# Two loads of one tile pair placed apart in the SyncE queue of a long-convolution and soft-MoE kernel

## The chip, the cores and the metric

The kernel runs on one core of one Trainium2 chip. The metric is device time of one launch in microseconds (us). Before the change three runs took 909.78, 915.08 and 910.25 us; their median is 910.25 us.

## What is computed

The input `x` has 8 batches of 5696 positions and 128 channels. It is convolved along the positions with a filter `h` as long as the sequence (in the reference by a Fourier transform of twice the length, causal part kept); the result, 45568 rows of 128, goes through a soft mixture of experts with 32 slots.

```python
def _attn_ref(x, h):
    L = 2 * S
    Xf = np.fft.rfft(x, n=L, axis=1)
    Hf = np.fft.rfft(h, n=L, axis=0)
    y = np.fft.irfft(Xf * Hf[None, :, :], n=L, axis=1)[:, :S, :]
    return y

def _moe_ref(x, phi, w1, w2):
    logits = x @ phi
    d = softmax(logits, axis=0)
    slot_input = (d.T @ x).reshape(E, S_per_e, D)
    for e in range(E):
        slot_out[e] = np.maximum(slot_input[e] @ w1[e], 0.0) @ w2[e]
    c = softmax(logits, axis=1)
    return c @ slot_out
```

(The two `softmax` calls stand for the reference's maximum, exponential and sum.) All arithmetic is 32-bit floating point.

## The kernel before, in words

The transform is done by matrix products in two levels, 90 by 64. Nine groups are run through it: group 0 is the filter, groups 1 to 8 are the batches. Between the levels the data goes through internal tensors in DRAM, because the axis that lies across the partitions changes.

- **Stage a** (`stage_a`, matmuls L241, evictions L243): folds and transforms eight chunks a group. It is called once a step for the low 60 frequencies and in every odd step also for the high 30 of two chunks. Its stores go to `f` (L225): two of 240 KB for the low part ("f60" below) and four of 120 KB for the high part ("f30" below). The input comes by `load_x` (tile `xc`, 768 KB, L198).
- **Stage b** (`load_g` L270, `stage_b1` L284, `stage_b2` L327 and L332): twelve units a group. A unit is loaded as `gt` (512 KB), transformed, multiplied by the filter's spectrum, transformed back and evicted as `zst`. The first eight units of a group are stored to `zm` (two stores of 256 KB), the last four to `zr` (four stores of 128 KB, or of 32 KB for the very last one). `load_g` of a group can run only when all of that group's `f` is written.
- **Stage c** (`stage_c1` to `stage_c6`): pairs of chunks, four pairs a batch, 32 in all. Pair T needs two loads: `load_main` brings 64 of the 90 frequencies (tile `zc` from `zm`, 1 MB, L374), `load_rest` the other 26 (tile `zx` from `zr`, 512 KB, L385). In `stage_c1` the matmuls of L412 read `zc`, and directly behind them on TensorE the matmuls of L417 read `zx` and add to the same banks. There is one buffer of each for the steady part. What follows from a pair are token rows, logits, both softmaxes and the accumulation of the slots' inputs.

**The order is written out by hand.** One loop over steps t = 0 to 80 issues for every step a piece of stage a, one to two units of stage b and a piece of stage c, and each engine runs its instructions in the order in which the loop issued them. `LAG_C` = 27: `stage_c1` of pair T is in the odd step 27 + 2T. `pair(-2)` in an odd step is the pair whose `stage_c1` comes two steps later, `pair(-1)` in an even step the pair whose `stage_c1` comes in the next step. `NQ` = 4, so `T % NQ == 0` is the first pair of a batch, whose `zr` data is written late.

**All steady loads and stores are issued by SyncE, in one queue.** Stores are not issued where they arise: `stage_a` and `stage_b2` append them to `pending`, and `flush()` issues what is there. Every DMA of the program takes the next of eight completion semaphores in turn and, before it is issued, waits for the DMA that used this semaphore eight DMAs earlier. SyncE is held meanwhile, with all that is queued behind.

In an odd step the queue gets: the two f60 stores (first `flush()`), `zc` of the pair two steps on, `zx` of the same pair directly behind it (unless it is the first of a batch), a `gt`, the stores of one unit, the four f30 stores (last `flush()`). In an even step: `zx` if the pair is the first of a batch, `xc`, the two f60 stores, `gt`, the stores of one unit (L225), a small store `c_t` (L562), another `gt`, the stores of another unit. After step 80 a tail without stages a and b runs the last pairs, the experts and the output.

Of the kernel before, what the change touches and what calls it, by code (L numbers as in the profile page):

```python
# [70 lines left out]
def kernel(  # L71
# [41 lines left out]
    NQ = NJ // 2  # L113
# [53 lines left out]
    def bank():  # L167
        rings.append(rings.pop(0))
        return rings[-1].tile([P, 512], F32, name="bank", tag="bank")
# [39 lines left out]
    def fold(c):  # L209
        if c not in xs:  # L210
            return
        t_ = xs.pop(c)
        y_ = xf[c % len(xf)]
        i = CH * (c % 2)
        near, far = t_[:, 0, i:i + CH, :], t_[:, 1, ::-1, :][:, i:i + CH, :]
        for o in range(2):
            nc.gpsimd.tensor_tensor(out=y_[:, o, :, :], in0=near, in1=far,  # L217
                                    op=AL.subtract if o else AL.add)
        folded[c] = y_
# [3 lines left out]
    def flush():  # L223
        while pending:
            pending.pop(0)()  # L225
# [38 lines left out]
    def load_g(u):  # L264
        if u >= (B + 1) * NW:
            return
        g, w, us = parts(u)
        n = sum(k for _, k in us)
        t_ = bpool.tile([P, 4, 2, D], F32, name="gt", tag="gt", bufs=3)
        nc.sync.dma_start(  # L270
            out=t_[:, 0:n, :, :].rearrange("p q c d -> p q (c d)"),
            in_=fd[g][8 * w:8 * w + 2 * n].rearrange("(q a) r c d -> (a r) q (c d)", a=2))
        gs[u] = t_
# [42 lines left out]
    def stage_b2(u):  # L316
        g, w, us = parts(u)
        if g == 0:
            return
        m = len(us)  # L320
        y_ = prods.pop(u)
        bz = bps.tile([P, 2, 2, 2 * D], F32, name="bz", tag="bz")
        for o, (i, n) in enumerate(us):
            for q in range(n):
                r = slice(q * HP, (q + 1) * HP)
                for a in range(2):
                    nc.tensor.matmul(bz[a * HP:(a + 1) * HP, q, o, :], vt[r, i, a, :],  # L327
                                     y_[r, a * m + o, :, :].rearrange("p c d -> p (c d)"),
                                     start=True, stop=True)
        n = us[0][1]  # L330
        st = bpool.tile([P, 2, 2, 2 * D], F32, name="zst", tag="zst", bufs=3)
        nc.scalar.activation(st[:, 0:m, 0:n, :].rearrange("p o q x -> p q o x"),  # L332
                             bz[:, 0:n, 0:m, :], AF.Copy)
        k = m * n
        sv = st[:, :, :, :].rearrange("p o q x -> p (o q) x")
        for o in range(2):
            if 8 * w < MAIN:
                pending.append(partial(
                    nc.sync.dma_start,
                    out=zm[g - 1][o, 8 * w:8 * w + 2 * k].rearrange("(q a) r c d -> (a r) q (c d)", a=2),  # L340
                    in_=sv[o::2, 0:k, :]))
                continue
            k0 = 8 * w - MAIN
            for c in range(2):
                pending.append(partial(
                    nc.sync.dma_start,
                    out=zr[g % 2][o, c, k0:k0 + 2 * k].rearrange("(q a) r d -> (a r) q d", a=2),
                    in_=sv[o::2, 0:k, c * D:(c + 1) * D]))
# [30 lines left out]
    def load_rest(T):  # L379
        if T >= NT:  # L380
            return
        b, j = divmod(T, NQ)
        t_ = zs[T]
        n = 2 * CH
        nc.sync.dma_start(  # L385
            out=t_[1][:, :, :, :].rearrange("p h n d -> p (h n d)"),
            in_=zr[(b + 1) % 2].rearrange("o c k r d -> (o c k) r d")[:, j * n:(j + 1) * n].rearrange(
                "p r x -> p (r x)"))
# [46 lines left out]
    def stage_c2(T):  # L435
        for k in (3, 1, 0, 2) if tail else (3, 2, 1, 0):
            p = bank()
            for i in range(CH):
                nc.tensor.transpose(p[:, i * TR:(i + 1) * TR], ys[T][0:TR, k * CH + i, 0:D],  # L439
                                    ident[0:TR, 0:TR])  # L440
            nc.scalar.activation(yt[:, k * CH:(k + 1) * CH, :, :], of_tokens(p), AF.Copy)  # L441
# [78 lines left out]
    def dispatch(T):  # L520
        ap_ = bank()
        d_ = ds.pop(T)
        y_ = ys.pop(T)
        for i in range(CH):
            for k in range(Q):
                r = slice(k * NSL, (k + 1) * NSL)
                nc.tensor.matmul(ap_[r, 0:D + 1], d_[:, i, r], y_[:, k * CH + i, :],  # L527
                                 start=(i == 0), stop=(i == CH - 1))
        if T == 0:
            nc.vector.tensor_copy(out=acc[:, :], in_=ap_[:, 0:D + 1])  # L530
        else:
            nc.vector.scalar_tensor_tensor(out=acc[:, :], in0=acc[:, :],
                                           scalar=scales.pop(T)[:, 0:1], in1=ap_[:, 0:D + 1],
                                           op0=AL.mult, op1=AL.add)
# [68 lines left out]
    def units(t):  # L603
        g, i = divmod(t - LAG_B, NJ)
        if t < LAG_B or g > B:
            return []
        return [g * NW + k for k in range(sum(PER[:i]), sum(PER[:i + 1]))]
# [23 lines left out]
    for t in range(last_front + 1):  # L631
        us = list(units(t))

        def pair(lag):
            T, half = divmod(t - LAG_C - lag, 2)
            return T if half == 0 and 0 <= T < NT else None

        def prefetch(last):
            nonlocal loaded
            while loaded < len(queue) and queue[loaded][0] <= last \  # L640
                    and queue[loaded][0] // NW * NJ + NJ <= t:
                load_g(queue[loaded][0])
                loaded += 1

        def slot_b(due=True):
            fresh = due and bool(us)
            if fresh:
                u = us.pop(0)
                stage_b1(u)
                prefetch(u + AHEAD)  # L650
                wait_b2.append(u)
            if len(wait_b2) > fresh:
                stage_b2(wait_b2.pop(0))

        T, U, V, W, X = [pair(k) for k in (0, 2, 1, 3, 5)]
        if t < NA:
            stage_a(t, False)
            fold(t + 1)
        if t == last_front:
            assert T is None and U is None  # L660
            assert pair(-1) % NQ
            flush()
            dispatch(W)
            for i in range(3):
                slot_b()
                flush()
                if i == 1:
                    softmax_sum(W)
                    stage_c2(V)
            assert not us and not wait_b2  # L670
            stage_c6(X)
            stage_c3(V)
            column_max(V)
            break
        if t % 2:
            if T is not None:
                stage_c1(T)()
            flush()
            if pair(-2) is not None:
                load_main(pair(-2))  # L680
                if pair(-2) % NQ:
                    load_rest(pair(-2))
            slot_b()
            if U is not None:
                stage_c4(U)
            if t < NA:
                stage_a(t, True)
            if U is not None:
                stage_c5(U)
                softmax_exp(U)  # L690
            flush()
        else:
            if pair(-1) is not None and pair(-1) % NQ == 0:
                load_rest(pair(-1))
            if t < NA:
                load_x(t // 2 + 2)
            flush()
            if t == NJ:
                prefetch(AHEAD - 1)
            slot_b()  # L700
            if W is not None:
                softmax_sum(W)
                dispatch(W)
            flush()
            if V is not None:
                stage_c2(V)
            if X is not None:
                stage_c6(X)
            slot_b()
            if V is not None:  # L710
                stage_c3(V)
                column_max(V)
            flush()
        if t == NA:
            lead.close()
            wts = inner.enter_context(tc.tile_pool(name="wts", bufs=1, side="right"))
            w1s = wts.tile([P, E, F], F32, name="w1s")
        if NA < t <= NA + E:
            nc.sync.dma_start(out=w1s[:, t - NA - 1, :], in_=moe_w1[t - NA - 1])
# [213 lines left out]
```

## Time and profile before

| | |
|---|---|
| three runs | 909.78, 915.08, 910.25 us; median 910.25 |
| profiled execution, own time | 909.23 us |
| its span in the trace | 907.4 us |
| granted TensorE clock, mean | 0.903 of full speed |
| TensorE matmul | 760.2 us busy, 84% of the span, 8308 instructions |
| TensorE weight load | 387.7 us, 43% |
| VectorE | 601.4 us, 66% |
| ScalarE | 436.8 us, 48% |
| GpSimd | 399.8 us, 44% |
| DMA, SyncE's and ScalarE's queue | 275.74 MB, 89.7% of 16 engines' span |
| DMA, all | 278.33 MB, mean 307 GB/s |

The profiled execution is one run of the program; its span leaves out 1.8 us around the first and last instruction. A view of the trace gives for every instruction its start, its duration and, in square brackets, how long its engine was idle before it and who ended that. For SyncE, the duration is that of the issue, not of the transfer. A piece "DMA" in the chain of waits runs from the issue to the landing.

### The profile page before, as it was taken

How to read it: one execution, taken by the hardware profiler on the slowest of the kernel's cores; microseconds unless marked ns; L12 is line 12 of the kernel's file. 1: busy time of each engine (PE TensorE's matmuls, PEld its weight loads, DVE VectorE, ACT ScalarE, POOL GpSimd, SP SyncE). 2: the span in 40 equal slices, each digit the busy share in tenths (PEclk: the TensorE clock that was granted, in tenths of full speed). 3: DMA queues.
4: the chain of work that ended last, by engine and by line, in shares of the span. 5: the costliest groups of instructions: out<-in, count | busy, mean ns of one | idle time of the engine just before them, and what ended most of it. 6: DMA issues, size and time to landing. Idle time of an engine off the chain costs nothing.

```text
span 907.4 us, 21291 instructions
## 1 busy us (share of the span) xinstructions
PE 760.2 (84%) x8308; PEld 387.7 (43%) x8308; DVE 601.4 (66%) x896; ACT 436.8 (48%) x880; POOL 399.8 (44%) x353
## 2 busy tenths in 40 slices
PE   6857778689999989999998999799888877767893
PEld 2212233234444444444444444344444434344793
DVE  2029767568778867886877787678778766653552
ACT  2423234335556545665655655456544444563441
POOL 4634322444555655655655566456332224651000
PEclk9979889999999999999999999899988888766855
DMA  8989999999999999999999999999998768540798
GB/s 267 318 275 343 293 296 337 298 314 376 341 291 375 361 326 308 372 358 299 357 364 335 295 373 348 303 308 346 306 291 304 264 200 341 186 166 1 292 406 335
DMA packets 170443, 278.33 MB, mean 307 GB/s; under 512 B 13543, under 2 KB 128231, under 8 KB 165135
## 3 DMA queue, kind: packets, MB, share of 16 engines
q1 hardware_dynamic: 169336, 275.74, 89.7%
q10 hardware_dynamic: 1008, 1.25, 0.5%
q8 instruction: 66, 1.08, 0.5%
q14 instruction: 33, 0.27, 0.1%
HBM read 147.94 MB, written 129.00 MB: 305 GB/s over the span
## 4 chain that ended last, share of the span: by engine, by line
PE 47%; DMA 23%; ACT 8%; POOL 8%; DVE 6%; issue 6%; SPq 1%; ACTq 0%; DVEq 0%; POOLq 0%
PE bank L241 9%; DMA gt<-f 9%; PE bt L284 9%; PE bz L327 6%; POOL y L430 5%; PE bank L412 4%; DMA f<-fst 4%; PE op L886 3%; PE bank L439 3%; PE bank L417 3%; PE bank L448 2%; DMA zx<-zr 2%; ACT fst L243 2%; DMA out_dram<-o 2%; PE bank L527 2%
## 5 line engine op out<-in xcount | busy, mean ns | idle before, releaser
L241 PE MATMUL bank<-x,s 128*32 128x512 f32 (+1 forms) x1152 | 218.0, 620 | 12.9 <-POOL x L217 8.4
L217 POOL TENSOR_TENSOR x<-xc 128x512 f32<-128x512 f32 x144 | 180.4, 1278 | 107.2 <-PE bank L241 86.5
L284 PE MATMUL bt<-gt,wt 64*64 64x256 f32 x1620 | 125.0, 419 | 72.8 <-DMA gt<-f 33.0
L430 POOL TENSOR_TENSOR y<-y,op 128x512 f32<-128x512 f32 x64 | 77.6, 1213 | 206.8 <-DVE op L404 204.3
L304 DVE TENSOR_TENSOR pi<-bt,Hi 128x1024 f32<-128x1024 f32 x96 | 113.0, 1177 | 83.5 <-PE bt L284 83.3
L243 ACT ACTIVATE fst<-bank 128x512 f32<-128x512 f32 x216 | 122.8, 592 | 86.0 <-PE bank L241 57.7
L332 ACT ACTIVATE zst<-bz 128x1024 f32<-128x1024 f32 x96 | 93.3, 972 | 128.3 <-PE bz L327 109.4
L284 PEld LDWEIGHTS bt<-gt,wt 64*64 64x64 f32 x1620 | 58.3, 141 | 151.2 <-issue 79.1
L312 DVE TENSOR_TENSOR yf<-bt,pi 128x512 f32<-128x512 f32 x192 | 119.4, 663 | 3.3
L304 DVE TENSOR_TENSOR bt<-bt,Hr 128x1024 f32<-128x1024 f32 x96 | 113.0, 1177 | 0.0
L241 PEld LDWEIGHTS bank<-x,s 128*32 128x32 f32 (+1 forms) x1152 | 55.1, 126 | 129.8 <-issue 93.6
L327 PE MATMUL bz<-yf,vt 64*64 64x256 f32 x1440 | 110.4, 404 | 0.0
L327 PEld LDWEIGHTS bz<-yf,vt 64*64 64x64 f32 x1440 | 64.3, 143 | 25.5 <-issue 4.2
L512 POOL TENSOR_TENSOR L<-L,rs 128x512 f32<-128x512 f32 x32 | 33.5, 1048 | 91.6 <-DVE rs L511 66.4
L404 DVE TENSOR_TENSOR y<-bank,y 128x512 f32<-128x512 f32 x32 | 22.1, 692 | 76.7 <-ACT y L420 76.5
L439 PE MATMUL bank<-ident,y 109*128 109x109 f32 x512 | 62.7, 273 | 7.9 <-ACT yt L441 7.9
L504 ACT ACTIVATE L<-L 128x512 f32<-128x512 f32 x32 | 20.2, 630 | 94.7 <-POOL L L501 94.6
L430 POOL TENSOR_TENSOR y<-y,om 128x512 f32<-128x512 f32 x54 | 63.9, 1183 | 2.1
L439 PEld LDWEIGHTS bank<-ident,y 109*128 109x128 f32 x512 | 52.9, 149 | 19.4 <-POOL x L217 14.7
L412 PE MATMUL bank<-zc,im 64*64 64x512 f32 x480 | 60.8, 623 | 0.0
L441 ACT ACTIVATE yt<-bank 128x360 f32<-128x360 f32 x128 | 53.0, 482 | 7.7 <-PE bank L439 7.3
L420 ACT ACTIVATE y<-bank 128x512 f32<-128x512 f32 x32 | 19.1, 596 | 72.6 <-PE bank L417 72.6
(101 smaller groups left out, 862.5 us busy)
## 6 DMA issues: line engine op xcount, KB each, us to landing
gt<-f SPq DMA_DIRECT2D x99, 512.0 KB
f<-fst SPq DMA_DIRECT2D x144, 240.0 KB
zm<-zst SPq DMA_DIRECT2D x128, 256.0 KB
zc<-zm SPq DMA_DIRECT2D x30, 1024.0 KB
xc<-in_x_dram SPq DMA_DIRECT2D x32, 768.0 KB
f<-fst SPq DMA_DIRECT2D x144, 120.0 KB
out_dram<-o SPq DMA_DIRECT2D x16, 1024.0 KB
zx<-zr SPq DMA_DIRECT2D x30, 512.0 KB
```

The lines of the kernel that those rows point to most:

```text
L217: nc.gpsimd.tensor_tensor(out=y_[:, o, :, :], in0=near, in1=far, op=AL.subtract if o else AL.add)
L241: nc.tensor.matmul(p[i * m:(i + 1) * m, :], s1[:, g // B, q + o, cols], columns(c_, o), start=True, stop=True)
L243: nc.scalar.activation(st[:, :, q, :], p[:, :].rearrange("p (n d) -> p n d", d=D), AF.Copy)
L284: nc.tensor.matmul(bt[q * HP:(q + 1) * HP, a, o, :], wt[r, 2 * i + q, :], t_[r, 2 * o + q, :, :].rearrange("p c d -> p (c d)"), start=True ...
L304: nc.vector.tensor_tensor(out=p_, in0=pv, in1=h_, op=AL.mult)
L312: nc.vector.tensor_tensor(out=y_[r, 0:k, c, :], in0=pv[:, :, c, :], in1=pi[r, 0:k, 1 - c, :], op=op_)
L327: nc.tensor.matmul(bz[a * HP:(a + 1) * HP, q, o, :], vt[r, i, a, :], y_[r, a * m + o, :, :].rearrange("p c d -> p (c d)"), start=True, sto ...
L332: nc.scalar.activation(st[:, 0:m, 0:n, :].rearrange("p o q x -> p q o x"), bz[:, 0:n, 0:m, :], AF.Copy)
L412: nc.tensor.matmul(ps[o, c][h_ * HP:(h_ + 1) * HP, :], im[r, c, :], zt[r, h_, :, c, :], start=True, stop=False)
L430: eng.tensor_tensor(out=part_, in0=part(v, 0), in1=o_[:, :, :], op=sign)
L439: nc.tensor.transpose(p[:, i * TR:(i + 1) * TR], ys[T][0:TR, k * CH + i, 0:D], ident[0:TR, 0:TR])
L441: nc.scalar.activation(yt[:, k * CH:(k + 1) * CH, :, :], of_tokens(p), AF.Copy)
```

## The change

Two loads change their place in the step; their number, size and data do not.

- `load_main` in an odd step is now issued directly after `stage_c1`, ahead of the `flush()` that issues the two f60 stores.
- `load_rest` is no longer issued behind it. It is issued for all pairs alike in the following even step, after the `flush()` that issues the stores of that step's first unit, so behind `xc`, two f60 stores, `gt` and the unit's stores, and ahead of `c_t` and the second `gt`. In the step that opens a group there are two `gt` ahead of it.
- In the last step (t = 80), which has its own order, `load_rest` stands after `dispatch`.

```diff
@@ -661,6 +661,7 @@
             assert pair(-1) % NQ
             flush()
             dispatch(W)
+            load_rest(pair(-1))
             for i in range(3):
                 slot_b()
                 flush()
@@ -675,11 +676,9 @@
         if t % 2:
             if T is not None:
                 stage_c1(T)()
-            flush()
             if pair(-2) is not None:
                 load_main(pair(-2))
-                if pair(-2) % NQ:
-                    load_rest(pair(-2))
+            flush()
             slot_b()
             if U is not None:
                 stage_c4(U)
@@ -690,8 +689,6 @@
                 softmax_exp(U)
             flush()
         else:
-            if pair(-1) is not None and pair(-1) % NQ == 0:
-                load_rest(pair(-1))
             if t < NA:
                 load_x(t // 2 + 2)
             flush()
@@ -702,6 +699,8 @@
                 softmax_sum(W)
                 dispatch(W)
             flush()
+            if pair(-1) is not None:
+                load_rest(pair(-1))
             if V is not None:
                 stage_c2(V)
             if X is not None:
```

## The prediction

> **What bounds the kernel now.** I read the page's slices first, to find the stage that the change touches. The two moved loads run from 176 us (pair 0) to 770 us, slices 8 to 34 of 40.
>
> ```profile
> PE   6857778689999989999998999799888877767893
> ...
> DMA  8989999999999999999999999999998768540798
> ```
>
> TensorE and the DMA engines are both over 90% busy in slices 8 to 29. So neither name alone settles anything: the question is which waits for the other, and where. TensorE's waits between 170 and 665 us, then SyncE's own from 176 to 665 us (total, times, longest):
>
> ```profile
> PE bt L284 <- DMA gt<-f: 16.2, 6, 5.5
> ...
> PE bank L417 <- DMA zx<-zr: 2.5, 2, 2.3
> ```
>
> ```profile
> SPq L225 <- DMA gt<-f: 40.3, 47, 2.4
> SPq L225 <- DMA zc<-zm: 22.1, 22, 1.7
> ```
>
> TensorE loses 16.2 us to `gt` (each time the first one of a group) and 2.5 us to `zx` (2.28 of it at pair 0). SyncE mostly waits for landings eight DMAs back: its queue is full, and runs behind the data that it stores. How far behind, a regular pair shows (pair 10, whose matmuls of L417 need `zx`). Three timelines: ScalarE, SyncE, TensorE.
>
> ```profile
> 378.58 1.06 ACT L243 ACTIVATE fst<-bank 128x512 f32<-128x512 f32 x2
> ```
>
> ```profile
> 383.20 3.99 SPq L225 DMA_DIRECT2D f<-fst  x4
> 388.22 0.34 SPq L198 DMA_DIRECT2D xc<-in_x_dram  x1
> 389.61 1.44 SPq L225 DMA_DIRECT2D f<-fst  x2
> 391.14 0.41 SPq L270 DMA_DIRECT2D gt<-f  x1
> 391.64 1.64 SPq L225 DMA_DIRECT2D zm<-zst  x2
> 393.38 0.57 SPq L562 DMA_DIRECT2D c_t<-cst  x1
> ...
> 398.17 0.34 SPq L374 DMA_DIRECT2D zc<-zm  x1
> 398.91 0.43 SPq L385 DMA_DIRECT2D zx<-zr  x1
> ```
>
> ```profile
> 391.62 1.95 PE L412 MATMUL bank<-zc,im 64*64 64x512 f32 x16
> 393.50 1.11 PE L417 MATMUL bank<-zx,ir 26*64 26x512 f32 x16
> ```
>
> The f30 data is evicted at 378.58 + 1.06 = 379.64, its first store goes out at 383.20: 3.6 us behind, and 7.2 at the fourth. The chain of waits gives a landing in that stretch, from issue to end:
>
> ```profile
> 391.64 6.46 DMA zm<-zst
> ```
>
> Last, what a group's first `gt` costs, at its worst (TensorE's timeline):
>
> ```profile
> 583.22 1.99 PE L284 MATMUL bt<-gt,wt 64*64 64x256 f32 x16 [5.52 <-DMA gt<-f]
> ```
>
> **Part 1: `zc` ahead of the f60 stores.** No instruction is added. The two stores' bytes no longer land before it, so it lands about 1.2 us earlier (neighbouring landings of f60 lie 0.6 us apart). In pairs 0 to 27 it landed 3.0 us or more before L412 used it (landings: last step of the DMA's completion semaphore): gain 0. The new wait: SyncE now stands at `zc` until L412 of the pair before has read the buffer, and the f60 stores, `gt` and unit stores queue behind. In the rows above that wait is long over at the issue (L412 ran at 371.5, `zc` of pair 10 was issued at 378.8), so 0; with SyncE level with TensorE it is up to 1.6 us (f60 evicted 372.2, L412 done 373.4, 0.4 of issue), and nobody needs those stores before the f30 stores behind them: still 0.
>
> **Part 2: `zx` moved on.** In pair 10's step its new place is behind the second `zm` store. As the queue is full, what lands by a place is set by the bytes ahead of it. Ahead of the new place stands what stood ahead of that store before, `zx` included, so `zx` will land about when that store landed: 398.85 us. L417 needs it at 393.50: 5.35 late. The same subtraction for pairs 0 to 23 gives 3.4 to 9.3 us late (pair 0: 197.68 against 190.13, 7.55; pairs 1 to 7: 4.2 to 7.1; pair 16: 7.9; pair 19: 9.3; pair 20: 7.0; pair 23: 3.7), and 0.8 to 11 us to spare for 24 to 27, step 80 among them: 0 there.
>
> These latenesses don't add up. Once TensorE has waited about 7 us at pair 0, everything it makes comes 7 us later while the queue, which was that far behind, goes on. So **pair 0 costs 7.0 us** (6.5 if `zx`'s own wait for the last `zr` stores, about 1 us, is gained; 7.55 if not). Then SyncE is level with the data, and what counts is the shortest path from eviction to L417. Regular pair, zero at 379.64, L417 due at 13.86: four f30 issues of 0.44 (two unheld ones took 0.88), `xc` issued by 2.3 and landed 5.5 later (shortest such row: 325.61 to 331.13), 7.8; two f60 (evicted at 5.2, no hold), 0.6 each, 9.0; `gt` 1.4, 10.4; two `zm` of 0.65, 11.7; `zx` 1.3, **13.0**. It fits by 0.9: **regular pairs 0**. In the step that opens a group (pairs 3, 7, 11, 15, 19) there is a second `gt` and four `zr` of 0.36 stand for the two `zm`: 14.5 against 13.4, **1.1 late, five times, 5.5 us**. Bounds by `xc`: 6.3 if it lands 2.75 (its spacing to its predecessor) after the last f30 at 3.5, which leaves nothing late; 7.0 after its issue, as in long queues, which makes 2.6 late, and regular pairs 0.6.
>
> **What goes.** A TensorE that is late by several us finds the groups' first `gt` there. The stalls after pair 0 were 3.36, 2.07, 1.69 and 5.52: **-12.6 us**. Before the worst of them the delay left is 7.0 + 4 x 1.1 - 3.36 - 2.07 - 1.69 = 4.3, and pair 19's row asks for 9.3; 5.0 is open. The queue may have caught up by then (0) or not (5.0); I take 2.0, nearer to caught up, since a regular cycle holds about 18.9 us of transfers by their landing spacing, against TensorE's 20.15. Removed with `zx` from its old place: `xc` or a unit's stores no longer wait behind it; with TensorE the later one, 0.
>
> **What other DMAs pay.** Moved behind `zx` are `c_t` and the step's second `gt`, 1.3 us later at most; `gt` is loaded three units ahead, and outside group starts no wait for it is recorded: 0.
>
> Sum: 7.0 + 5.5 - 12.6 + 2.0 = **+1.9 us** on the profiled execution's 909.2 us, 911.1. The median of the runs is 1.0 above that execution: **912**.
>
> A rule of the Trainium skill speaks against the change: "DMA: Bandwidth & Descriptors", Rules for kernel authors, has a DMA issued early and waited for late, and `zx` is now issued some 13 us later; taken alone it would have every pair pay, where the rows make only pair 0 and group starts pay. The same page (Anatomy of one DMA) fits a DMA on GpSimd's path as 2.0 us plus bytes at 436 GB/s; as an estimate for `xc` that is 3.8 us where the rows have 5.5 and more, no pair but the first would be late, and the sum would be about -6.
>
> **Rivals.** (a) *The shortest path does not fit*: `zx` lands later than 13.86 us after the f30 eviction in regular pairs too. It decides from 0.9 us of extra latency on, such as `xc` rows of 7 us. One us late in 18 regular pairs and 2.1 at five group starts: 18 + 10.5 + 7.0 - 12.6 + 2.0 = +25, 935. For it: `xc` rows reach 7.1. Against: those stood in a full queue.
> (b) *It fits everywhere*: 6.5 + 0 - 12.6 + 0 = -6, 904. For it: the shorter landing of `xc`.
> (c) *No pair is late*, because the queue, with no two loads side by side, is never behind: the 2.3 us of pair 0 go, and 1.3 us at each of four `gt` stalls: -7.5, 903. For it: the DMA engines moved only 133 GB/s from 345.5 to 350 us, where `zx` waited for `zr`. Against: 24 rows that say late.
> (d) *The queue keeps the pace it had, and TensorE just follows*: pair 20's row, with no `gt` stall after it, leaves +7.0 at the end, 917. It is the upper part of the forecast, not a case apart.
>
> **How the numbers follow.** Forecast 0.57, (a) 0.23, (b) 0.15, (c) 0.05. A measurement of this kernel can tell about 1% from no change, 9.1 us. (b), (c) and nearly all of the forecast lie within it: faster 0.04, same 0.69, slower 0.27 ((a) and the forecast's bad end, boundaries at 2.6 and the 5.0 open). The range goes from (b), 904, to 926, which takes in the forecast's bad end and the milder half of (a): about 0.07 is left out below and 0.11 above.
>
> **What the profile of after would show.** TensorE's wait for `zx` at L417 grows from 2.5 us to 12 to 16: one wait of about 9 at pair 0 and about 1 at five group starts; more than 15 such waits mean (a), none means (c). The wait of L284 for `gt` falls from 16.2 to under 6. SyncE waits more for evictions (L243, L332) and less for `zc` and `gt` landings. From pair to pair L412 comes every 20.15 us. Wrong from the root would be: `zx` landing in its new place well before the store ahead of it did, or a period over 20.15 without a wait for a DMA.

## The result and the profile after

The changed kernel takes 1008.2 us (median of four runs, 1008.15 to 1008.72); the kernel before, run beside it, 910.01 (four runs, 908.73 to 915.08). The ratio is **1.107, 95% interval 1.103 to 1.111**: 98 us slower, where 912 was forecast with a range to 926. The profiled execution of the changed kernel has a span of 1006.4 us against 907.4, and a mean granted clock of 0.88 against 0.903.

The slices of the changed kernel's page, the same two rows as before:

```profile
PE   5758677678888878887988798878987877766893
...
DMA  8999999988888888888888888798888986652598
```

In slices 8 to 29 TensorE was at 9 in 16 of 22 and is now in 3; the DMA engines were in all 22 and are now in one. Both have become less busy at once, so neither is short of time: they wait for each other. TensorE's waits of the changed kernel between 170 and 665 us, then SyncE's between 176 and 665 us (total, times, longest):

```profile
PE bank L417 <- DMA zx<-zr: 75.9, 19, 6.8
...
PE bt L284 <- DMA gt<-f: 1.4, 1, 1.4
```

```profile
SPq L225 <- ACT L L479: 54.5, 14, 7.0
SPq L198 <- POOL x L217: 45.4, 19, 4.3
SPq L270 <- PE bt L284: 45.4, 16, 5.3
SPq L225 <- ACT fst L243: 18.8, 22, 2.0
SPq L225 <- DMA gt<-f: 7.3, 7, 2.2
```

The wait for `zx` grew from 2.5 to 75.9 us and comes once in nearly every pair; the groups' stalls for `gt` fell from 16.2 to 1.4. SyncE's waits for landings (40.3 and 22.1 us before) have shrunk to 7.3 and 1.7, and in their place stand waits for the engines. One of them the prediction never mentions: L198, the issue of `xc`, waits 19 times for GpSimd's L217, the fold that reads the `xc` buffer. The waits of the first and third line, for an eviction (the view names L479; the unit store below starts at 303.66, as ScalarE's L332 ends) and for the buffer of `gt`, come earlier in each pair and are over when `xc` waits.

One pair of the changed kernel that does not border a group's start, between two matmul groups of L417 on TensorE, then GpSimd and SyncE in between (three timelines):

```profile
296.91 2.02 PE L417 MATMUL bank<-zx,ir 26*64 26x512 f32 x16 [3.86 <-DMA zx<-zr]
...
322.08 1.12 PE L417 MATMUL bank<-zx,ir 26*64 26x512 f32 x16 [2.94 <-DMA zx<-zr]
```

```profile
301.70 2.44 POOL L430 TENSOR_TENSOR y<-y,op 128x512 f32<-128x512 f32 x2 [10.90 <-DVE op L404]
304.10 2.45 POOL L430 TENSOR_TENSOR y<-y,om 128x512 f32<-128x512 f32 x2
306.61 1.05 POOL L501 TENSOR_TENSOR L<-L,rm 128x512 f32<-128x512 f32 x1
307.62 2.51 POOL L217 TENSOR_TENSOR x<-xc 128x512 f32<-128x512 f32 x2
```

```profile
303.66 1.25 SPq L225 DMA_DIRECT2D zm<-zst  x2
306.06 1.67 SPq L225 DMA_DIRECT2D f<-fst  x4
310.15 0.34 SPq L198 DMA_DIRECT2D xc<-in_x_dram  x1
310.59 0.84 SPq L225 DMA_DIRECT2D f<-fst  x2
311.55 0.63 SPq L270 DMA_DIRECT2D gt<-f  x1
312.28 2.29 SPq L225 DMA_DIRECT2D zm<-zst  x2
314.92 0.36 SPq L385 DMA_DIRECT2D zx<-zr  x1
```

Read them as one circle. L417 of a pair ends its banks; VectorE's folding of them (L404) releases GpSimd's L430 at 301.70; behind four such operations and L501, in GpSimd's own order, stands the fold L217, which ends at 310.13; 0.02 us later SyncE, which had nothing to issue since 307.73, issues `xc`; and the moved `zx` stands behind it with five DMAs in between, issued at 314.92, landed at 322.04. At 322.08 the next pair's L417 starts. So `zx` of a pair now depends on L417 of the pair before, and by this reading the circle sets the period: 24.8 us, where it was 20.15.

The chain of waits, asked for the same stretch, does not draw this circle. Its last pieces:

```profile
312.40 0.39 PE bank L551 x4
312.79 0.02 issue
312.81 0.48 ACT cst L561
313.29 0.60 SPq L225
...
314.92 7.12 DMA zx<-zr
```

It goes from `zx` back to a store (L225) that it believes released by ScalarE's L561, and from there along TensorE's own work. That store does not read what L561 writes, and its issue had begun at 312.28, before L561 ended at 313.29, so the link is a doubtful one; whether the fold or TensorE's work holds `zx` was left to the experiments.

### The profile page after: what moved, and what is told of

Its sections match the earlier page's. It is cut to its first block, busy times and chain, and to the rows that moved or that the text cites. A ratio compares the mean times of both kernels' runs of the same rounds, so it can differ in the third digit from the quotient of the medians.

```text
span 1006.4 us, 21258 instructions
## 1 busy us (share of the span) xinstructions
PE 790.2 (79%) x8308; PEld 395.8 (39%) x8308; DVE 603.0 (60%) x896; ACT 439.4 (44%) x880; POOL 399.9 (40%) x353
## 4 chain that ended last, share of the span: by engine, by line
PE 44%; DMA 29%; ACT 6%; POOL 5%; issue 5%; SPq 5%; DVE 4%; ACTq 0%; DVEq 0%; POOLq 0%
DMA zx<-zr 16%; PE bank L241 9%; PE bt L284 9%; PE bz L327 6%; DMA f<-fst 5%; PE bank L417 4%; SPq L225 4%; PE bank L439 3%; POOL y L430 3%; DMA gt<-f 3%; DMA out_dram<-o 3%; PE bank L527 2%; PE op L885 2%; DMA xc<-in_x_dram 2%; PE bank L412 2%
## 5 line engine op out<-in xcount | busy, mean ns | idle before, releaser
L217 POOL TENSOR_TENSOR x<-xc 128x512 f32<-128x512 f32 x144 | 180.3, 1278 | 108.2 <-PE bank L241 84.0
L430 POOL TENSOR_TENSOR y<-y,op 128x512 f32<-128x512 f32 x64 | 77.5, 1211 | 299.5 <-DVE op L404 297.0
L284 PE MATMUL bt<-gt,wt 64*64 64x256 f32 x1620 | 137.1, 453 | 57.5 <-issue 32.5
L304 DVE TENSOR_TENSOR pi<-bt,Hi 128x1024 f32<-128x1024 f32 x96 | 112.9, 1176 | 82.7 <-PE bt L284 82.1
L243 ACT ACTIVATE fst<-bank 128x512 f32<-128x512 f32 x216 | 123.1, 592 | 90.1 <-PE bank L241 56.5
L332 ACT ACTIVATE zst<-bz 128x1024 f32<-128x1024 f32 x96 | 93.3, 972 | 135.8 <-PE bz L327 118.1
L404 DVE TENSOR_TENSOR y<-bank,y 128x512 f32<-128x512 f32 x32 | 22.1, 692 | 174.4 <-ACT y L420 174.2
L312 DVE TENSOR_TENSOR yf<-bt,pi 128x512 f32<-128x512 f32 x192 | 119.3, 663 | 3.3
L284 PEld LDWEIGHTS bt<-gt,wt 64*64 64x64 f32 x1620 | 62.1, 151 | 148.1 <-issue 93.4
L327 PE MATMUL bz<-yf,vt 64*64 64x256 f32 x1440 | 119.1, 430 | 0.0
L417 PE MATMUL bank<-zx,ir 26*64 26x512 f32 x480 | 44.9, 810 | 87.3 <-DMA zx<-zr 87.3
L304 DVE TENSOR_TENSOR bt<-bt,Hr 128x1024 f32<-128x1024 f32 x96 | 113.0, 1177 | 0.0
L327 PEld LDWEIGHTS bz<-yf,vt 64*64 64x64 f32 x1440 | 68.8, 154 | 31.0 <-issue 11.1
L430 POOL TENSOR_TENSOR y<-y,om 128x512 f32<-128x512 f32 x54 | 64.0, 1186 | 2.1
L412 PE MATMUL bank<-zc,im 64*64 64x512 f32 x480 | 60.3, 618 | 0.0
L441 ACT ACTIVATE yt<-bank 128x360 f32<-128x360 f32 x128 | 53.2, 476 | 10.4 <-PE bank L439 10.2
```

Source lines behind the costliest of these rows:

```text
L243: nc.scalar.activation(st[:, :, q, :], p[:, :].rearrange("p (n d) -> p n d", d=D), AF.Copy)
L284: nc.tensor.matmul(bt[q * HP:(q + 1) * HP, a, o, :], wt[r, 2 * i + q, :], t_[r, 2 * o + q, :, :].rearrange("p c d -> p (c d)"), start=True ...
L304: nc.vector.tensor_tensor(out=p_, in0=pv, in1=h_, op=AL.mult)
L312: nc.vector.tensor_tensor(out=y_[r, 0:k, c, :], in0=pv[:, :, c, :], in1=pi[r, 0:k, 1 - c, :], op=op_)
L412: nc.tensor.matmul(ps[o, c][h_ * HP:(h_ + 1) * HP, :], im[r, c, :], zt[r, h_, :, c, :], start=True, stop=False)
L417: nc.tensor.matmul(p[h_ * HP:(h_ + 1) * HP, :], ir[r, :], zx[r, h_, :, :], start=False, stop=True)
```

## The experiments

Five readings were set against each other. **P**: the circle above, closed because `zx` stands behind `xc`. **Q**: `zx` is late because of the bytes ahead of it in full DMA queues. **R**: part 1 (`zc` ahead of the f60 stores) does it. **B**: it is the f60 and unit stores ahead of `zx` that count, since they wait for evictions, and not `xc`. **C**: the lower clock does it.

All results in one table. Times are medians, ratios are to the kernel before on the same chip. "Period", and the issues of `xc` and `zx` (start of the issuing instruction, counted from the start of the previous pair's L417), are medians over the pairs that do not border a group's start; the waits are TensorE's totals between 170 and 665 us. The kernel before took 913.4 us beside e1 to e4, 917.5 beside e5 to e8, 914.1 beside e9 to e11 and 912.2 beside e12; across these groups the ratios are the ones to compare.

| kernel | us | ratio (95%) | period | `xc` issued | `zx` issued | wait for `zx` | wait for `gt` |
|---|---|---|---|---|---|---|---|
| before | 910.0 | 1 | 20.15 | 15.17 | 6.95 | 2.5 | 16.2 |
| changed | 1008.2 | 1.107 (1.103 to 1.111) | 24.81 | 12.80 | 17.39 | 75.9 | 1.4 |
| e1 | 905.9 | 0.991 (0.987 to 0.995) | 20.15 | 14.96 | 6.75 | 1.1 | 9.2 |
| e8, same as e1 | 909.2 | 0.992 (0.990 to 0.995) | 20.15 | 15.75 | 7.07 | 2.1 | 10.7 |
| e2 | 1001.0 | 1.097 (1.089 to 1.105) | 24.41 | 12.62 | 17.49 | 73.0 | 1.0 |
| e3 | 920.6 | 1.009 (1.005 to 1.013) | 20.20 | 15.01 | 13.58 | 1.9 | 22.1 |
| e4 | 958.4 | 1.049 (1.043 to 1.055) | 21.74 | 15.67 | 14.80 | 54.8 | 0 |
| e5 | 992.6 | 1.085 (1.077 to 1.092) | 24.23 | 12.37 | 16.93 | 22.2 | 0 |
| e6 | 925.8 | 1.012 (1.005 to 1.019) | 20.76 | 12.37 | 12.86 | 21.7 | 8.4 |
| e7 | 950.6 | 1.039 (1.034 to 1.045) | 20.90 | 15.70 | 15.02 | 23.4 | 18.0 |
| e9 | 1069.0 | 1.168 (1.158 to 1.177) | 27.37 | 15.95 | 20.62 | 72.8 | 0 |
| e10 | 910.0 | 0.998 (0.994 to 1.002) | 20.15 | 15.38 | 7.26 | 0.2 | 8.6 |
| e11 | 989.9 | 1.081 (1.075 to 1.087) | 23.82 | 15.04 | 2.94 | 0 | 2.4 |
| e12 | 954.6 | 1.041 (1.030 to 1.053) | 21.41 | 8.49 | 14.89 | 46.1 | 0 |

**Which part: e1 and e8 (part 1 alone), e2 (part 2 alone).** The diffs in this section are against the changed kernel; e1 puts `load_rest` back to where it was, only with the f60 stores ahead of it:

```diff
             flush()
+            if pair(-2) is not None and pair(-2) % NQ:
+                load_rest(pair(-2))
             slot_b()
...
         else:
+            if pair(-1) is not None and pair(-1) % NQ == 0:
+                load_rest(pair(-1))
...
-            if pair(-1) is not None:
-                load_rest(pair(-1))
```

> Part 1 of the change alone: zc ahead of the two f60 stores, zx behind these stores and otherwise where it was. Theory P (a loop closed by zx: L417 of one pair, ScalarE, VectorE and GpSimd, the fold that frees the buffer of xc, the issue of xc, and behind it in SyncE's queue the f60 stores, gt, the unit's stores and zx, then L417 of the next pair; 25 us long in the profile after): zx is not behind xc, so 907 to 913 us. Theory Q (zx is late because of the bytes ahead of it in a full DMA queue, whoever releases them): the bytes ahead of zx are as before, 907 to 913. Theory R (part 1 does it: SyncE stands at zc until L412 has read the buffer, and all stores and loads queue behind): over 950 us, up to 1008.

e2 puts the f60 stores back ahead of `zc`:

```diff
+            flush()
             if pair(-2) is not None:
                 load_main(pair(-2))
-            flush()
```

> Part 2 alone: zc behind the f60 stores as before the change, zx where the change puts it. Theories P and Q: all of the loss, 1000 to 1012 us, a wait of L417 for zx of 3 to 6 us in each of pairs 1 to 20. Theory R: 907 to 920 us.

R falls: part 2 alone costs 9.7%, and part 1 alone makes the kernel faster, by 0.9% (1 us below what P and Q expected). Since that is a small gain, e1 was timed again, as e8:

> Part 1 alone once more, with more rounds: the f60 stores between zc and zx, nothing else changed against before. If the gain of the first time was real, a ratio of 0.985 to 0.996; if it was the spread of this kernel's runs, an interval that takes in 1.

It came out the same, 0.992. TensorE's waits in e1 show a part of it, in the same window as above:

```profile
PE bt L284 <- DMA gt<-f: 9.2, 4, 3.6
```

That is 7.0 us less than before (5.5 less in e8), and the wait for `zx` is 1.4 us less. But waits for VectorE and ScalarE that the kernel before did not have take most of it back: all of TensorE's waits that the view lists in that window add up to 38.1 us before, 35.9 in e1 and 35.8 in e8. So these waits show some 2 of the 7 to 8 us; where the rest comes from stays open.

**What closes the circle: the place of `zx` against `xc`, the stores and `gt`.** e3 issues `zx` first in the even step, ahead of `xc` (`load_rest(pair(-1))` moved to the head of the `else:` branch).

> zc as the change has it, zx one place earlier than xc: first in the even step for every pair, so still apart from zc. Theory P: zx no longer stands behind the load that waits for GpSimd, and lands where only the first pairs of a batch had it before: 903 to 913 us, waits for zx under 5 us in all. Theory Q: 9.0 us of transfers fewer ahead of it (xc 2.75, two f60 1.2, gt 1.4, unit's stores 1.3, and their latency), so also near before, 905 to 920. Theory R: over 950 us.

The period is back at 20.20 us and TensorE waits 1.9 us for `zx`, as P has it. Yet the time missed P's 903 to 913 by 8 us: `zx` now stands ahead of the groups' first `gt`, and that wait is 22.1 us where e1 has 9.2. Q expected 905 to 920 here, so e3 does not tell P from Q.

e4 leaves `zx` where the change put it and moves `xc` directly behind it:

```diff
-            if t < NA:
-                load_x(t // 2 + 2)
             flush()
...
             if pair(-1) is not None:
                 load_rest(pair(-1))
+            if t < NA:
+                load_x(t // 2 + 2)
```

> zc and zx as the change has them, but xc is issued directly behind zx instead of first in the even step: zx stays behind f60, gt and the unit's stores, and only the load that waits for GpSimd's fold is gone from ahead of it. Theory P: the loop through GpSimd is cut; zx follows the unit's stores, whose data is ready 7.75 us before L417 needs zx, and two issues and a landing of 4 to 6 us fit in that: 905 to 925 us, granted clock at 0.5 in few pairs. Theory Q (bytes): xc's 2.75 us of transfer per pair go from ahead of zx, at most 21 x 2.75 = 58 us gained: 950 us or more. Theory R: over 950 us.

This missed P by 33 us. The kernel became 50 us faster, so half of the loss does go with `xc`; as a time it lies in Q's range too (950 or more). A period of 21.74 us with a wait for `zx` in every pair says what P had left out: a second circle was behind the first. SyncE's largest wait in e4 names it, then ScalarE in the pair whose L417 starts at 404.75:

```profile
SPq L225 <- ACT fst L243: 38.9, 36, 2.4
```

```profile
415.20 0.63 ACT L504 ACTIVATE L<-L 128x512 f32<-128x512 f32 x1 [2.02 <-POOL L L501]
415.74 1.07 ACT L243 ACTIVATE fst<-bank 128x512 f32<-128x512 f32 x2
```

The f60 stores that stand ahead of `zx` wait for their eviction, and that ends 11.5 us after the start of L417 in most pairs (12.06 in this one), because ScalarE's L243 there stands behind L504, which waits for GpSimd's L501, and so again for L430. Add 3.3 us up to the issue of `zx` (14.80) and 7.2 from there to its landing: 22.0, about the period measured. So B is half right: the stores close a circle too, a shorter one.

e6 takes the stores and `gt` away from between (`zx` directly behind `xc`), e7 takes `xc` and `gt` away (the even step issues f60, `zx`, `xc`, `gt`, unit's stores):

```diff
             if t < NA:
                 load_x(t // 2 + 2)
+            if pair(-1) is not None:
+                load_rest(pair(-1))
             flush()
...
-            if pair(-1) is not None:
-                load_rest(pair(-1))
```

> zx directly behind xc, ahead of the even step's f60 stores, gt and unit's stores. It still waits for GpSimd's fold through xc. Theory P: from L417 to the end of the fold that frees xc 12.3 to 13.2 us, two issues 0.9, landing of xc and zx together 6 to 7: 19.2 to 21.1 against a period of 20.15; waits of 0 to 1 us a pair and the groups' first gt late behind zx: 915 to 935 us. Theory B (what counts is the f60 eviction and the unit's stores ahead of zx, not xc): 905 to 915.

```diff
         else:
+            flush()
+            if pair(-1) is not None:
+                load_rest(pair(-1))
             if t < NA:
                 load_x(t // 2 + 2)
-            flush()
...
-            if pair(-1) is not None:
-                load_rest(pair(-1))
```

> Even step in the order f60 stores, zx, xc, gt, unit's stores. Theory P with the second loop that the run with xc behind zx showed (L417 to the eviction of the even step's f60 12.1 us, then issues, then the landing): 12.1 + 1.2 of issues + 4 to 5 of landing = 17.3 to 18.3 against 20.15, so no pair is late; the groups' first gt goes out behind zx and xc, as where zx was first: 912 to 930 us. If the place behind any store of the step is enough to be late: 945 and more.

e6 came within P's bounds, and B's 905 to 915 did not come. With `xc` at 12.37, `zx` goes out at 12.86 instead of 17.39 and lands 6.95 later, as a median 0.6 us before L417 needs it; of the 21.7 us of waits for it, 20.2 are at pair 0 and behind the five group starts.

e7 came out as the second branch of its expectation, 951, so P's first branch missed. Its period is only 0.75 us above 20.15, and TensorE's waits for `zx` and `gt` are together 22.7 us more than before, of some 35 us lost; the rest was not taken apart. `zx` goes out at 15.02, not at the 13.3 that the expectation reckoned with (12.1 and 1.2 of issues): so near the old period SyncE again mostly waits for landings eight DMAs back, as it did before, and one of them is new. `zc`, whose eighth DMA back is now `xc`, is held for it (two lines of SyncE's waits):

```profile
SPq L225 <- DMA gt<-f: 42.4, 56, 1.3
...
SPq L374 <- DMA xc<-in_x_dram: 13.3, 13, 2.8
```

e10 keeps `zx` in the odd step, apart from `zc`, but behind the first `gt`, so that the fold, `xc` and the even step's stores are all behind it (the first pair of a batch and the even step are as in e1):

```diff
             slot_b()
+            if pair(-2) is not None and pair(-2) % NQ:
+                load_rest(pair(-2))
             if U is not None:
                 stage_c4(U)
```

> Part 1 as changed, and zx of a regular pair stays in the odd step, but behind the first gt there (zc, f60 stores, gt, zx, unit's stores, f30 stores); a group's first pair as before. So no two loads of a pair stand together, and xc, the next step's stores and GpSimd's fold all stand behind zx. P: the loop through GpSimd is not closed, the period stays 20.15 us, no wait of TensorE for zx in regular pairs; the time is that of part 1 alone within 5 us: 902 to 914. If any place behind more than zc makes zx late, 920 or more.

It fits P: 20.15 us, 0.2 us of wait for `zx`. That two loads stand apart costs nothing. Against part 1 alone it gains nothing either. Since e3, e6 and e10 also take bytes from ahead of `zx`, they fit P but do not rule out Q.

**The clock: e5** runs the matmuls of L412 three times over in pairs 0 to 20, which fills TensorE's wait for `zx` with work.

```diff
-        for c in (1, 0):
+        for again in range(3 if T < 21 else 1):
+            for c in (1, 0):
...
-                                     zt[r, h_, :, c, :], start=True, stop=False)
+                                         zt[r, h_, :, c, :], start=True,
+                                         stop=again < (2 if T < 21 else 0))
```

> The changed kernel, but in pairs 0 to 20 the matmuls of L412 are run three times over (same operands, same banks, the sums begun anew each time): 3.76 us more of TensorE work just ahead of each wait for zx, which fills the wait. Theory P (the loop through GpSimd, xc and zx sets the period of 25 us): the added work lies in the wait, the clock stays up, L417 takes 1.1 us instead of 2.0 in the 13 or so pairs where it ran slow, and only these 0.9 us and some matmuls ahead of the next fold are gained: 985 to 1005 us. Theory C (the halved clock after each wait, 102 us of half clock between 190 and 700 us, is a cause of its own and half of the loss): 955 to 975 us. If TensorE's work were on the path as it is before the change, 21 x 3.76 = 79 us more, 1085.

The clock rose to 0.926, above that of before, and the period fell only to 24.23. C falls as the main cause: the clock is worth some 16 us of the 98 by the times, 20 by the ratios.

**GpSimd's part measured by itself: e9, e11, e12.** e9 moves one of GpSimd's two L430 pairs of operations to VectorE, in order to end the fold 2.45 us earlier; e11 does the same to part 1 alone, as a control.

```diff
-            for v, o_, eng in ((1, op, nc.gpsimd), (0, om, nc.vector if tail else nc.gpsimd)):
+            for v, o_, eng in ((1, op, nc.gpsimd), (0, om, nc.vector)):
```

> The changed kernel with one of GpSimd's two L430 operations (the one on om) moved to VectorE in all pairs; nothing in SyncE's queue is moved. P (each pair's period is a loop: matmuls of L417 -> VectorE -> GpSimd's L430, L501 and the fold L217 -> xc's issue -> the queue -> zx's landing -> the next L417): GpSimd's fold ends about 2.45 us earlier after L417, xc and zx follow it, and the period falls from 24.8 to about 22.4 us: 20 to 23 pairs x 2.45 = 49 to 56 us less, 950 to 965 us. Q (zx is late because of the bytes ahead of it in full DMA queues, and xc's wait for the fold only happens to end there): GpSimd's work does not matter, 1000 us or more. If VectorE's extra work delays evictions ahead of the loop's own, P gains less: up to 980.

> Part 1 alone, with the same L430 operation moved from GpSimd to VectorE: what that move is worth where zx is not late. P: GpSimd's fold does not set xc's issue there in regular pairs (xc is issued about 2.6 us after the fold's end, when its turn in the queue comes), so the period stays 20.15 us and the time is that of part 1 alone within 5 us: 900 to 912; VectorE's extra 1 to 2 us per pair may cost up to 10 if it delays evictions. A gain of more than 10 us would mean that GpSimd is a limit of its own and e9 says nothing on zx.

Both missed P's range, and by a lot: 1069 and 990; by the number alone e9 lies in Q's (1000 or more). But the edit did not do what it was for. VectorE needs 2.65 us for the moved operations and does them ahead of the unit's L304 and L312 and ahead of L500, which L501 waits for; so the fold ended later, 15.0 to 15.9 us after L417 instead of 12.8. e11 shows what that costs with `zx` early, in TensorE's waits between 200 and 665 us:

```profile
PE bt L284 <- DVE yf L312: 63.0, 20, 4.2
```

e9 tells something all the same: with the fold 3.1 us later, `zx` is issued 3.2 us later and lands 0.04 us before it is used, and the period grows by 2.56. Meanwhile DMA is less busy than in the changed kernel (mostly 7 in the slices), and `zx` lands 7.0 us after its issue, against 7.3. That fits P better than Q, but VectorE's own delay is mixed into it, so e9 settles nothing.

e12 therefore moves the fold forward in GpSimd's order, ahead of L430, and moves no work between the engines. The input's folded chunk needs a fourth buffer for that; the room comes from letting `lt` serve as `dt` too, with two tiny instructions a pair that reset its padding.

```diff
-    xf = [apool.tile([P, 2, CH, D], F32, name=f"x{i}", tag=f"x{i}", bufs=1) for i in range(3)]
+    xf = [apool.tile([P, 2, CH, D], F32, name=f"x{i}", tag=f"x{i}", bufs=1) for i in range(4)]
...
             fold(t + 1)
+            if t % 2:
+                fold(t + 2)
```

> The changed kernel with GpSimd's second fold (L217) of each pair ahead of the L430 operations instead of behind L430 and L501. For that stage a's folded input has a fourth buffer, and lt takes dt's place to make room (two tiny instructions a pair reset its padding). SyncE's order and VectorE's and GpSimd's work otherwise are as in the changed kernel. P: xc no longer waits for the fold; it is issued right behind the last f30 store, about 2 us earlier in the loop, and the f60 eviction, 12.1 to 12.4 us after L417, is the next limit. zx is issued 1.5 to 2.5 us earlier, the period falls from 24.8 to 22.3 to 23.3 us, the time by 23 x 1.5 to 2.5 = 35 to 58 us, to 950 to 973. Q (bytes ahead of zx decide): the fold only happens to end there, 995 or more. As SyncE's waits: L198's wait for GpSimd's L217 (46.9 us in the changed kernel) goes to under 5 by P; by Q the same time appears as waits for landings.

954.6, as P has it. GpSimd and SyncE around one such pair of e12, whose L417 starts at 303.50 (there the lines from 357 to some 450 are moved by two: L428 is L430 of the other kernels, L383 is L385; L502 is L501):

```profile
297.79 4.97 POOL L217 TENSOR_TENSOR x<-xc 128x512 f32<-128x512 f32 x4
307.39 2.45 POOL L428 TENSOR_TENSOR y<-y,op 128x512 f32<-128x512 f32 x2 [4.63 <-DVE op L402]
309.81 2.44 POOL L428 TENSOR_TENSOR y<-y,om 128x512 f32<-128x512 f32 x2
312.30 1.05 POOL L502 TENSOR_TENSOR L<-L,rm 128x512 f32<-128x512 f32 x1
```

```profile
310.21 2.70 SPq L225 DMA_DIRECT2D f<-fst  x4
313.18 0.89 SPq L198 DMA_DIRECT2D xc<-in_x_dram  x1
315.01 0.77 SPq L225 DMA_DIRECT2D f<-fst  x2
315.89 0.66 SPq L270 DMA_DIRECT2D gt<-f  x1
316.64 2.14 SPq L225 DMA_DIRECT2D zm<-zst  x2
318.84 0.62 SPq L383 DMA_DIRECT2D zx<-zr  x1
```

Both folds are over at 302.76, and `xc` is issued at 313.18, directly behind the f30 stores and while GpSimd's L502 still runs; no wait of L198 for L217 is left among SyncE's waits. What took its place is the second circle, that of e4, as SyncE's waits between 176 and 665 us have it:

```profile
SPq L225 <- ACT fst L243: 54.5, 41, 3.0
```

18.8 in the changed kernel, 54.5 here. The same bytes stand ahead of `zx` in the same order, and it goes out 2.5 us earlier after L417: Q, which expected 995 or more, falls as the main cause. The link to L561 falls too: in most such pairs of e12 the second unit store goes out 13.9 to 14.2 us after L417, before that instruction (L562 there) ends at 14.35.

Not tried: a third buffer for `xc`.

## Why the prediction was wrong

**The step that failed is "`xc` issued by 2.3" in the shortest path of a regular pair, and with it "regular pairs 0".** The path was put together from SyncE's issues and DMA landings alone, as if nothing but the queue held `xc`. Here it is again with what was measured, counted from the end of the f30 eviction (medians over the pairs that do not border a group's start; as in the forecast, "issued" is the end of the issuing instruction, and a landing is the last step of the DMA's completion semaphore):

| | forecast | changed kernel | e12 |
|---|---|---|---|
| `xc` issued | 2.3 | 4.83 | 2.15 |
| `xc` landed | 7.8 | 10.44 | 7.82 |
| f60 landed | 9.0 | 11.74 | 9.27 |
| `gt` landed | 10.4 | 14.06 | 11.54 |
| `zm` landed | 11.7 | 15.40 | 13.14 |
| `zx` landed | 13.0 | 16.64 | 14.52 |
| L417 could start | 13.86 | 13.11 | 13.53 |

Of the 3.6 us that `zx` is late against the path, 2.5 are the issue of `xc`, 0.9 is `gt` (2.3 us behind f60, not 1.4), and all other spacings were right within 0.1. And TensorE is ready 0.75 us sooner than the trace of before had it, because the eviction that the count starts from itself comes later after L417 (7.92 us, 6.29 before); so `zx` is 3.5 us late in each pair instead of 0.9 early. In e12, where the fold is out of the way, `xc` is issued and landed as forecast, and the time is 54 us less than the changed kernel's (60 by the ratios). Its pairs are still 1.0 us late: that is the second mis-sized term, `gt`, with 2.3 us behind f60 there too.

The trace of before held the number. GpSimd's timeline there, in the very step that the prediction took its zero from (f30 evicted at 379.64):

```profile
382.16 1.05 POOL L501 TENSOR_TENSOR L<-L,rm 128x512 f32<-128x512 f32 x1
383.16 2.53 POOL L217 TENSOR_TENSOR x<-xc 128x512 f32<-128x512 f32 x2
```

The fold ended at 385.69, 6.05 us after the zero. It cost nothing then, because `xc`'s turn in the full queue came at 388.22, 2.5 us later, so no wait showed in this pair. With the fold's 6.05 and 0.35 of issue, 6.4 in place of 2.3, the prediction's own sum has regular pairs 13.0 + 4.1 - 13.86 = 3.2 late and group starts 1.1 + 4.1 = 5.2; over 18 and 5 of them, 58 + 26 + 7.0 - 12.6 + 2.0 = +80, 990 us. The prediction looked at what the queue waited for, not at what it would wait for once it ran level.

**The clock was not priced at all.** By e5 it is worth 16 to 20 us, and `gt`'s 0.9 us in each of 23 pairs would be 21. Together they are more than the 18 us that the sum still lacks, so it does not close to the microsecond. The clock is told in the last section.

The other steps:

- *Pair 0 costs 7.0*: L417 of pair 0 ran at 197.38 instead of 190.13, 7.25. The number fits, in part by luck: its L412 already ran 2.7 us later than before (188.64 instead of 185.91; 1.1 of it stood at 172 us already, ahead of the moved loads), and the wait for `zx` there grew by 4.5, from 2.28 to 6.79.
- *A TensorE that is late finds the groups' first `gt` there, -12.6*: right, 16.2 fell to 1.4, and the one left is ahead of pair 0.
- *Group starts 1.1 late, pair 19 open by 2.0*: neither exists by itself, since the circle makes every pair late.
- *Part 1: gain 0*: too low. Part 1 alone is 0.8 to 0.9% faster. Its stalls for `gt` are shorter, but most of that comes back as other waits, and e10, with almost the same stalls in its profile, took 0.2% less than before (interval from 0.6% less to 0.2% more). Why part 1 gains is not shown.
- *Both TensorE and the DMA engines over 90% busy in slices 8 to 29*: the DMA engines were; TensorE was below 90% in 6 of the 22.
- *SyncE waits more for evictions (L243, L332)*: so for L332 (the line under the name of L479), hardly for L243 (17.5 to 18.8 us).
- *`zc` and the second `gt`: 0*: right, no wait of L412 for `zc` is listed, and one wait for `gt`.
- *Rival (a), "the shortest path does not fit"*, was the case, and its sign came as named: more than 15 waits for `zx`. It was priced at one us a pair, +25; the pairs paid 4.7 each in period. It had the right row to doubt, `xc`, but for its landing (5.5 forecast, 5.6 measured) and not for its issue.

The rule of the Trainium skill that the prediction set against its rows ("DMA: Bandwidth & Descriptors", Rules for kernel authors: issue early, wait late) has the right sign here: every pair paid, +4.66 us of period. But e3 issues `zx` 6.6 us later than the kernel before and has a period of 20.20, so the runs do not tie the loss to a late issue as such. The fit on the same page (Anatomy of one DMA), made for GpSimd's path, gives 3.2 us for the 512 KB of `zx`, an estimate. On SyncE's queue the medians from the start of the issue to the landing were 7.3 us in the changed kernel and 5.9 to 7.2 in the other kernels that issue it in the even step.

The best kernel found is part 1 alone, 0.991 and 0.992 of the time before.

## What to carry to other kernels

Before a load is moved back in an in-order issuing queue, list every instruction that it is moved past, with the engine that releases its buffer, and read from the trace when that release *comes*, not only whether anyone waits for it now: a full queue hides a release that is 2.5 us early and becomes the bound when the queue runs level. If any of them is released by work that follows from the matmul which the load feeds one round before, the load is tied into a circle, and the circle's length is the new period. And a second circle may stand behind the first (e4, e12), so an edit that cuts one is to be read from the period, not from the wait that went away.

## What the runs showed of the hardware

TensorE's granted clock fell to half after most waits of a few us: in the changed kernel around 19 of the 21 waits for `zx` in pairs 0 to 20, not around those of 1.67 and 2.50 us. Three stretches of the pair shown above, busy time of the engines and the clock; the first follows a wait of 3.86 us, the third one of 2.94:

```profile
296.90:302.50 5.60, 5.59 (x49) 2.14 (x49) 2.83 (x5) 1.08 (x2) 0.80 (x1) 0.50 0.97 376
302.50:322.00 19.50, 16.65 (x184) 8.26 (x180) 13.25 (x20) 11.15 (x22) 10.94 (x10) 0.98 0.83 260
322.00:327.00 5.00, 4.92 (x51) 2.59 (x52) 3.05 (x5) 1.65 (x3) 1.02 (x1) 0.66 1.03 405
```

For 5.6 us the clock is at 0.50 (the figure ahead of the last two), and the sixteen matmuls of L417 take 2.02 us instead of the 1.11 that they took in the kernel before. The stretches at half clock that begin between 190 and 700 us add up to 102 us in the changed kernel and to 34 in the kernel before. The page "TensorE: Matmul & The Clock Gate" of the Trainium skill (What's actually happening) has the rate halved after an idle window of about 3.4 us and restored after a busy one as long. The runs agree on the length (the half-clock stretches of the changed kernel last 3.41, 6.83 or 10.24 us, and their starts lie whole multiples of 3.41 us apart), but less idle time was enough: the wait of 2.94 us did it, and in the kernel before stalls of 2.07 and 2.28. In the 3.41 us right ahead of a start in the changed kernel TensorE was idle for 1.86 us or more. Because L430 waits for these matmuls, the half clock also lengthens the circle that causes it: where L417 took 2.01 us the fold ended 13.2 us after its start, where it took 1.12, 12.3.
